# Attention and two MLPs on one core: the second MLP's first layer by seven half products, and one list schedule for both MLPs

## The chip, the cores and the metric

One core of one Trainium2 chip runs the whole program in one launch. The metric is device microseconds (us) of that core. The core has five engines with a queue each, worked off in order: TensorE (PE, matmuls, with weight loads as PEld), VectorE (DVE), ScalarE (ACT), GpSimd (POOL) and SyncE (SP, which issues the DMAs here). Matmuls write PSUM, eight banks of 128 partitions x 512 floats; GpSimd works on SBUF alone.

## The reference

q, k and v are float32; the weights come as float64, in words of 8 bytes, which the kernel turns into floats itself.

```python
attn_out = softmax(q @ k.T / 8, causal) @ v          # 2 batches, 12 heads, 448 tokens, 64 wide
x = attn_out as (896 tokens, 768)
g = x @ w_gate;  val = x @ w_val                     # 768 -> 1536
x2 = (g * sigmoid(g) * val) @ w_out                  # 1536 -> 768
h = x2 @ w_in                                        # 768 -> 2048, moe2_w_in
out = (h * clip(h + 3, 0, 6) / 6) @ moe2_w_out       # 2048 -> 768
```

## The kernel before

**Precision.** Every MLP operand is split in two parts of a reduced float type, a high one (CAST on ScalarE) and the rest (a subtraction on VectorE or GpSimd, `parts_of`). A product of two operands is then three matmuls: high x high, high x low, low x high (`mm3`). The weights come as float64 words: a load of 768 KB lands in `raw`, a Prelu on ScalarE turns the high words, a shift and a join on VectorE (`floats`) finish the float, and a split follows (`unit`).

**Stages.** Attention comes first (up to about 117 us). Then, in the transposed layout (features on partitions, tokens along the free axis, 448 tokens of each batch):

- *Gate and value layers of the first MLP.* Two blocks f of 128 features are done plainly (`plain`). The other ten go by Winograd's form of Strassen's method: the 2 x 2 block matrix has gate and value as its upper and lower half and the two halves of the 768 inputs as columns; the 2 x 2 block operand has the input halves as rows and the two batches as columns. In place of eight half products there are seven (`products`, 9 matmuls of 448 columns each). The weights' sums (s1 to s4) are made per block by `operands`, the tokens' sums (t1 to t4) once. The seven results are combined through sums in banks x, y, z, w and in SBUF tiles (u2, u3, v2), then SiLU and gate (`gate`).
- *w_out*, 432 matmuls: per 128 output features two banks, for tokens 0 to 383 and 384 to 895 (`PARTS`). The results are split into x2h, x2l.
- *w_in* of the second MLP, 16 blocks f of 128 features in plain form, 36 matmuls each: per block one bank of 384 and one of 512 columns; ScalarE makes the relu r, VectorE multiplies and splits (g2h, g2l).
- *w2_out*, two halves of 384 output features, 336 matmuls of 384 columns each: seven banks of 128 tokens, added up over 16 blocks; the last two pairs of blocks run token by token, so that copies and stores begin early.

**What sets the order.** From the plain blocks to w_out the operations are handed to a planner (`Plan.op`, with a cost per engine that may do it) and put in an order by a list schedule (`Plan.run`): the matmuls and the loads in the order written, everything else by when it can start and when the matmuls need it; where `vec` and `pool` may both do it, the schedule picks. Operations marked `port` (all inputs in SBUF) do not overlap each other in the plan. The emitted order is then fixed. w_in and w2_out are issued by loops behind the plan (`next_unit`, `last_layer`), ordered by the framework's own scheduler with raised priority for the work on a bank.

**Names in rows.** L53 is the helper through which all ordered engine calls go, so most rows have that line: go by tiles. `mm` is a PSUM bank, `x`, `t`, `x2` are token operands, `a`, `s` weight operands of the seven products, `whi`/`wlo` those of plain products, `tmp` the SBUF sums, `w`/`v` weights as floats, `gh`/`gl`, `g2h`/`g2l` the split gated results.

Of the kernel before, what the change touches and what calls it, by code (L numbers as in the profile page):

```python
# [8 lines left out]
F32 = mybir.dt.float32  # L9
# [25 lines left out]
EARLY = 0  # L35
SOON = 200
# [124 lines left out]
def tile_attention_glu_mlp(  # L161
# [126 lines left out]
    OUT_ORDER = [(0, 0), (1, 0), (0, 1), (1, 1)] + [(e, hh) for e in range(2, KD) for hh in range(2)]  # L288
    for e, hh in OUT_ORDER:
        rows = w_out[hh * KD * 128 : (hh + 1) * KD * 128]  # L290
        units.append((cols(rows, e), KD, 128))
    for f in range(K2):
        units.append((cols(w2_in, f), KD, 128))
    for eh in range(2):
        for g in range(K2 // 2):
            rows = w2_out[g * 256 : (g + 1) * 256]
            units.append((cols(rows, eh, EH), 2, EH))
# [5 lines left out]
    used = [0]  # L303

    def prefetch(n):
        while len(made) < min(n, len(units)):
            for step in w_unit(*units[len(made)]):
                step()

    def next_unit():  # L310
        u = used[0]
        prefetch(u + 1 + AHEAD)
        used[0] += 1
        got = made[u]
        made[u] = None
        return got

# [13 lines left out]

    PARTS = (slice(0, NT - 512), slice(NT - 512, NT))
# [326 lines left out]
    def mlps():  # L659
        in_attention.clear()  # L660
        more.append(ctx.enter_context(tc.tile_pool(name="more", bufs=1)))
        tmp = ctx.enter_context(tc.tile_pool(name="tmp", bufs=3))
# [3 lines left out]
        def whole(dt, name):  # L666
            return slot([128, NT], dt, name)

        def side(size, name):
            return tmp.tile([128, size], F32, tag=f"sg{size}", name=name, bufs=2 if size == 512 else 1)  # L670

        BATCH = [slice(b * S, (b + 1) * S) for b in range(B)]
        plan = Plan()
        PE448, PE384, PE512 = 0.2005, 0.1735, 0.2275
# [26 lines left out]
        def floats(src, name):  # L701

            raw = ring_spot("raw", [128, KD, 128, 2], U32, "raw")
            w = ring_spot("w", [128, KD, 128], F32, name)
# [63 lines left out]
        temps = [take([128, 2, S], F32, f"tmp{i}") for i in range(3)]  # L768
        ta, tb, sg = temps
# [4 lines left out]
        def gate(f, b, bank_, in0, in1):  # L774

            whole_f, hi, lo = g1[f]
            mid = lambda t: t[:, BATCH[b]]
            m = {"vec": 0.63}
            if whole_f is not None:
                combine(m, at(whole_f, b, mid), in0, in1, ALU.mult)  # L780
                return
            tok = lambda t: t[:, :S]
            combine(m, at(bank_, None, tok), in0, in1, ALU.mult)
            parts_of(at(bank_, None, tok), at(hi, b, mid), at(lo, b, mid), S, both=False, port=False)

        def g_tiles(f):
            if f < EARLY:
                g1[f] = None, take([128, NT], F32R, f"gh{f}"), take([128, NT], F32R, f"gl{f}")
            else:
                g1[f] = take([128, NT], F32, f"g{f}"), None, None  # L790

        def g_parts(f):
            src = g1[f][0]
            hi, lo = take([128, NT], F32R, f"gh{f}"), take([128, NT], F32R, f"gl{f}")
            for part in PARTS:
                mid = lambda t, part=part: t[:, part]
                parts_of(at(src, None, mid), at(hi, part.start, mid), at(lo, part.start, mid), part.stop - part.start)
            g1[f] = None, hi, lo
            give(src)

# [21 lines left out]
        def operands(f):  # L822

            wg, wv = floats(cols(w_gate, f), "w"), floats(cols(w_val, f), "v")
# [13 lines left out]
            combine(either, a21, a11, a21, ALU.subtract, port=True)  # L838
            piece("s3", a21)
# [3 lines left out]
            piece("a12", a12)  # L843
            combine(either, a12, a12, s2, ALU.subtract, port=True)
            piece("a22", a22)
# [3 lines left out]
        def unit(src, both=False):  # L849

            w = floats(src, "w")
            hi, lo = (ring_spot("ws", [128, KD, 128], F32R, n) for n in ("whi", "wlo"))
            parts_of(at(w), at(hi), at(lo), KD * 128, both=both)
            return hi, lo

        def plain(f, ws):

            g_tiles(f)
            for b in range(B):
# [13 lines left out]
                gate(f, b, got[1][0], at(got[1][0], None, tok), at(sg, b, nth(b)))  # L873
# [3 lines left out]
        used[0] += 2  # L877
        for f in range(1, PLAIN):
            plain(f, [unit(cols(w, f), both=True) for w in (w_gate, w_val)])
# [13 lines left out]
        p1, u2, u3, v2 = at(ta, 0, nth(0)), at(ta, 1, nth(1)), at(tb, 0, nth(0)), at(tb, 1, nth(1))  # L893
        add = {"vec": 0.63}
        for f in range(PLAIN, K1):
            a = operands(f)
            g_tiles(f)
            (x, nx), (z, nz), (y, ny), (w, nw) = (bank_spot() for _ in range(4))
            X, Y, Z, W = (at(t, None, tok) for t in (x, y, z, w))
            products(x, a["a11"], b11, True)  # L900
            plan.op(
                {"act": 0.54}, lambda e, x=x: e.copy(p1[2](ta()), tok(x())), reads=[x], writes=[p1[:2]]
# [21 lines left out]
        for f in range(EARLY, K1):  # L924
            g_parts(f)
        x2s = [tuple(take([128, NT], F32R, f"x2{p}{e}") for p in "hl") for e in range(KD)]
        pts = {}
        for u, (e, hh) in enumerate(OUT_ORDER):
# [18 lines left out]
            if hh == 0:  # L947
                continue
# [110 lines left out]
```

## Time and profile before

| | us |
|---|---|
| three runs | 601.73, 604.72, 604.35; median 604.35 |
| the profiled execution, whole | 602.2 |
| its span, first to last instruction | 600.4 |
| mean granted TensorE clock | 0.999 of full speed |

Busy time is given as a share of the span; engines overlap, so the shares add up to more than one, and matmuls are pipelined, so that a matmul's row is longer than the distance to the next. The chain of work that ended last is followed back from the last instruction; where a chain's piece is one engine alone, that engine was never waiting there.

### The profile page before, as it was taken

To read this page: it belongs to the slowest core of one execution; us is meant where nothing else is said; L and a number is where in the kernel's file an instruction comes from. 1 tells how busy PE (TensorE), PEld (TensorE's weight loads), DVE (VectorE), ACT (ScalarE), POOL (GpSimd) and SP (SyncE) were. 2 spreads that over 40 slices of the span, in tenths; PEclk is the share of its full clock that TensorE was granted. 3 is DMA by queue.
4 is the path that set the end of the run, shared out by engine and by line. 5 is a ranking of instruction groups with operands and counts; after the bars stand their busy time and mean duration, and the time that the engine had idled before them with its cause. 6 is when DMAs were issued, how large, how long until landed. Compare 5 with 4: busy or idle time off the path is not lost.

```text
span 600.4 us, 9398 instructions
## 1 busy us (share of the span) xinstructions
PE 593.0 (99%) x3528; PEld 551.0 (92%) x3528; DVE 372.3 (62%) x771; ACT 297.1 (49%) x536; POOL 176.7 (29%) x141
## 2 busy tenths in 40 slices
PE   8999999999999999999999999999999999999997
PEld 5999999989899999999999988888888899999997
DVE  6888889788999998879775434555555522223001
ACT  5788787775554555467344234555555532222000
POOL 4555555140343542363000012222222222223200
PEclk9999999999999999999999999999999999999999
DMA  9555546063333453342566333333343344341002
GB/s 180 131 136 131 133 116 176 7 204 106 105 107 106 149 161 111 106 139 76 163 201 211 105 106 106 105 106 105 106 109 109 108 128 120 112 136 62 1 0 94
DMA packets 83918, 70.15 MB, mean 117 GB/s; under 512 B 35232, under 2 KB 79776, under 8 KB 83872
## 3 DMA queue, kind: packets, MB, share of 16 engines
q1 hardware_dynamic: 83872, 69.55, 40.0%
q8 instruction: 28, 0.46, 0.3%
q14 instruction: 18, 0.15, 0.1%
HBM read 61.73 MB, written 2.75 MB: 107 GB/s over the span
## 4 chain that ended last, share of the span: by engine, by line
PE 94%; DVE 4%; ACT 1%; DMA 0%; issue 0%; POOL 0%; SPq 0%; ACTq 0%; DVEq 0%
PE mm L53 78%; PE pv L574 5%; PE sc L503 4%; PE tp L546 3%; PE tr L428 1%; DVE e L516 1%; DVE qq L441 1%; PE tr L608 1%; DMA kn<-in_k_dram 0%; POOL wlo L53 0%; DVE xn L587 0%; PE zero L367 0%; DVE et L552 0%; PE tr L458 0%; ACT L53 0%
## 5 line engine op out<-in xcount | busy, mean ns | idle before, releaser
L53 POOL TENSOR_TENSOR wlo<-w,whi 128x768 fp32r<-128x768 f32 (+1 forms) x33 | 59.1, 1791 | 257.5 <-PE mm L53 233.1
L53 DVE TENSOR_SCALAR w<-w 128x768 uint32<-128x768 uint32 (+1 forms) x59 | 35.6, 604 | 79.6 <-ACT w L53 76.6
L53 PE MATMUL mm<-whi,g2l 128*128 128x384 f32 x224 | 74.8, 334 | 0.0
L53 PE MATMUL mm<-whi,g2h 128*128 128x384 f32 x224 | 74.8, 334 | 0.0
L53 PE MATMUL mm<-wlo,g2h 128*128 128x384 f32 x224 | 74.8, 334 | 0.0
L574 PE MATMUL pv<-v,et 112*112 112x65 f32 x480 | 73.7, 242 | 0.0
L53 ACT CAST whi<-w 128x768 fp32r<-128x768 f32 (+1 forms) x49 | 40.1, 819 | 66.5 <-PE mm L53 57.4
L53 PE MATMUL mm<-x2h,wlo 128*128 128x384 f32 (+1 forms) x192 | 69.9, 364 | 0.0
L53 PE MATMUL mm<-x2l,whi 128*128 128x384 f32 (+1 forms) x192 | 69.8, 364 | 0.0
L53 PE MATMUL mm<-x2h,whi 128*128 128x384 f32 (+1 forms) x192 | 69.6, 362 | 0.0
L574 PEld LDWEIGHTS pv<-v,et 112*112 112x112 f32 x480 | 65.6, 177 | 1.2
L53 ACT ACTIVATE w<-raw 128x768 f32<-128x768 f32 (+1 forms) x59 | 52.5, 891 | 28.6 <-POOL wlo L53 19.4
L546 PE MATMUL tp<-ident,e 112*112 112x112 f32 x240 | 60.5, 260 | 1.7 <-ACT e L526 1.1
L526 ACT ACTIVATE e<-e,m 112x336 f32<-112x336 f32 (+1 forms) x96 | 48.8, 530 | 19.4 <-DVE m L516 18.4
L53 DVE SCALAR_TENSOR_TENSOR w<-raw,w 128x768 uint32<-128x768 uint32 (+1 forms) x59 | 57.3, 971 | 0.8
L53 PE MATMUL mm<-t,s 128*128 128x448 f32 x270 | 57.0, 366 | 0.0
L53 PEld LDWEIGHTS mm<-t,s 128*128 128x128 f32 x270 | 50.5, 188 | 4.9 <-DVE s L53 0.9
L53 PE MATMUL mm<-gh,wlo 128*128 128x384 f32 (+1 forms) x144 | 52.5, 364 | 0.0
L53 PE MATMUL mm<-gl,whi 128*128 128x384 f32 (+1 forms) x144 | 52.4, 364 | 0.0
L53 PE MATMUL mm<-gh,whi 128*128 128x384 f32 (+1 forms) x144 | 52.2, 362 | 0.0
L516 DVE CUSTOM_DVE_ANT_0 e<-sc,mask 112x336 f32<-112x336 f32 (+1 forms) x96 | 40.7, 446 | 5.2 <-PE sc L503 3.6
L53 PEld LDWEIGHTS mm<-whi,g2h 128*128 128x128 f32 x224 | 42.0, 188 | 0.0
(120 smaller groups left out, 1272.4 us busy)
## 6 DMA issues: line engine op xcount, KB each, us to landing
raw<-in_moe_w_out_dram SPq DMA_DIRECT2D x28, 768.0 KB, 4.3
raw<-in_moe_w_in_dram SPq DMA_DIRECT2D x16, 768.0 KB, 4.5
raw<-in_moe_w_gate_dram SPq DMA_DIRECT2D x12, 768.0 KB, 4.3
raw<-in_moe_w_val_dram SPq DMA_DIRECT2D x12, 768.0 KB, 5.9
kn<-in_k_dram SPq DMA_DIRECT2D x24, 112.0 KB, 2.6
qn<-in_q_dram SPq DMA_DIRECT2D x24, 112.0 KB, 2.7
v<-in_v_dram SPq DMA_DIRECT2D x12, 224.0 KB, 3.1
out_dram<-ob SPq DMA_DIRECT2D x14, 192.0 KB, 1.8
```

The lines of the kernel that those rows point to most:

```text
L53: ins = call(*args, **kw)
L428: nc.tensor.transpose(tr[:, c * C : (c + 1) * C], n[:, c].rearrange("p j d -> p (j d)"), ident[:C, :C])
L441: nc.vector.tensor_copy(hi[r, j, :], f[r, :])
L503: nc.tensor.matmul(sp[:C, o : o + w], t["qq"][:, j, c * C : (c + 1) * C], t[("kk", "k2")[i]][:, j, 0:w], start=(i == 0), stop=(i == 1),)
L516: nc.vector.tensor_tensor_reduce(out=es, in0=sp[:C, o : o + w], in1=mask[:, S - w :], op0=ALU.add, op1=ALU.min, scale=-SCALE, scalar=3.0e3 ...
L526: nc.scalar.activation(out=es, in_=es, func=AF.Exp, scale=-1.0, bias=m[:, x : x + 1])
L546: nc.tensor.transpose(tp[:C, at - lo : at - lo + C], e[:, at : at + C], ident[:C, :C])
L574: nc.tensor.matmul(box["o"][:, qc, :], et[:, at : at + C], vt[:, j, c, :], start=(c == 0), stop=(c == qc))
L608: nc.tensor.transpose(tr[:, c * C : (c + 1) * C], xn[:, c].rearrange("p j d -> p (j d)"), ident[:C, :C])
```

## The change

- **w_in by seven products.** Blocks 2f and 2f + 1 take the place of gate and value: 8 pairs of 7 products, each 9 matmuls of 448 columns. The sums t1 to t4 and the blocks b11, b21, b22 of x2 are made as w_out's banks end (`turned`), for which w_out's banks now hold 448 tokens of a batch each and its output blocks come in pairs e, e + 3. The gated results are kept as floats (`h`) and split later (`whole_parts`), since SBUF has no room for both parts beside the operands.
- **Sums in PSUM.** One function `seven` does both layers. ScalarE copies the first product from bank x into bank y, TensorE adds product s2 x t2 on top; ScalarE copies that sum to bank z and to u2, TensorE adds s3 x t3 and later a22 x t4 onto z. VectorE is left with two adds (W + u2, and v2 = Z + v2). The first product of the next block, a11, is issued between s3 and a22 of the present one.
- **One plan to the end.** w_in and w2_out, copies and stores are planned too. Four groups of w2_out's matmuls (`fill`) stand between s3 and a22 of the last pair.
- Splits may go to either engine in more places (`both`), and the splits of the first four gated blocks are let into the gate layers (`FEW`).

The core of the diff (the planner's class and attention are untouched):

```diff
+        def seven(n, source, sets, tiles, near, far, fill=None):
+
+            b11, b21, b22, (t1, t2, t3, t4) = *sets[:3], sets[3:]
...
+            ahead = begin(0)
+            for f in range(n):
+                a, x, nx = ahead
+                (y, ny), (z, nz), (w, nw) = (bank_spot() for _ in range(3))
+                Z, W = (at(t, None, tok) for t in (z, w))
+
+                def p6():
+                    products(y, a["s2"], t2, False)
+                    bank_copy(z, y)
+                    bank_copy(u2, y)
+
+                def p5():
+                    products(w, a["s1"], t1, True)
+                    bank_copy(v2, w)
+
+                bank_copy(y, x)
+                for step in (p5, p6) if f == 0 else (p6, p5):
+                    step()
+                products(x, a["a12"], b21, False)
+                near(f, x)
+                products(z, a["s3"], t3, False)
+                if f + 1 < n:
+                    ahead = begin(f + 1)
+                elif fill:
+                    idle.extend((nx, ny))
+                    fill()
+                combine(add, W, W, u2, ALU.add)
+                combine(add, v2, Z, v2, ALU.add)
+                products(z, a["a22"], t4, False)
+                far(f, 0, y, z)
+                products(w, a["s4"], b22, False)
+                far(f, 1, y, w)
...
-            products(x, a["a11"], b11, True)
...
-            products(z, a["s3"], tk[3], True)
-            products(y, a["s2"], tk[2], True)
-            combine(add, u2, Y, p1, ALU.add)
-            combine(add, u3, Z, u2, ALU.add)
-            products(w, a["s1"], tk[1], True)
-            combine(add, v2, W, u3, ALU.add)
-            products(x, a["a12"], b21, False)
-            silu(at(sg, 0, nth(0)), x)
-            products(z, a["a22"], tk[4], False)
-            combine(add, Z, Z, u2, ALU.add)
-            gate(f, 0, z, Z, at(sg, 0, nth(0)))
-            products(w, a["s4"], b22, False)
-            combine(add, W, W, u2, ALU.add)
...
+        def relu_far(f, b, y, t):
+            if b:
+                gated(2 * f, 1, at(sg, 0, nth(0)), at(t, None, tok))
+            else:
+                gated(2 * f + 1, 1, at(y, None, tok), v2)
+                gated(2 * f + 1, 0, at(sg, 1, nth(1)), at(t, None, tok))
...
+            lambda f: (cols(w2_in, 2 * f), cols(w2_in, 2 * f + 1)),
...
-        for f in range(K2):
-            wh, wl = next_unit()
...
-                mm3(pt, [(wh[:, i], wl[:, i], x2[i][0][:, part], x2[i][1][:, part]) for i in range(KD)])
```

Three places show how the order moves. The first is TensorE in w_in: before, a run of one block (its bank of 384 columns ends, its bank of 512 begins), and after, the same layer from a pair's product s3 to its a22. In the names `x` is a token operand there (x2, t or b blocks alike), `s` and `a` the weights' parts; the numbers tell buffers apart.

```order
L53 MATMUL mm_4183<-x2h_4029,whi 128x384
L53 MATMUL mm_4183<-x2l_4034,whi 128x384
L53 MATMUL mm_4183<-x2h_4029,wlo 128x384
L53 MATMUL mm_4207<-x2h_3575,whi 128x512
L53 MATMUL mm_4207<-x2l_3584,whi 128x512
L53 MATMUL mm_4207<-x2h_3575,wlo 128x512
```

```order
L52 MATMUL mm_4432<-x_3957,s_4332 128x448 x3
L52 MATMUL mm_4432<-x_4158,s_4332 128x448 x3
L52 MATMUL mm_4475<-x_3603,a_4400 128x448 x2
L52 MATMUL mm_4475<-x_3603,a_4400 128x448 [waits DVE_49]
L52 MATMUL mm_4475<-x_3787,a_4400 128x448 x3
L52 MATMUL mm_4475<-x_4059,a_4400 128x448 x3
L52 MATMUL mm_4432<-x_3730,a_4348 128x448 [waits DVE_49]
L52 MATMUL mm_4432<-x_3730,a_4348 128x448
L52 MATMUL mm_4432<-x_3730,a_4348 128x448 [waits Pool_49]
L52 MATMUL mm_4432<-x_3961,a_4348 128x448 x3
```

Bank 4432 (z) gets product s3, then bank 4475 the next pair's a11, then z again its a22, whose first matmul waits for VectorE; before, no matmul came back to a bank that another engine had to read first.

The second is VectorE in w_in: before, one block's gate and split between the conversions of the weights, and after, somewhat more than half of a pair's round.

```order
L53 SCALAR_TENSOR_TENSOR mm_4123<-r_4142,mm_4123 128x384 [waits Activation_49]
L53 TENSOR_TENSOR g2l_4122<-mm_4123,g2h_4121 128x384 [waits Activation_49]
L53 SCALAR_TENSOR_TENSOR mm_4147<-r_4166,mm_4147 128x512 [waits Activation_49]
L53 TENSOR_SCALAR w<-w 128x768 [waits Activation_49]
L53 TENSOR_TENSOR g2l_4122<-mm_4147,g2h_4121 128x512 [waits Activation_49]
L53 SCALAR_TENSOR_TENSOR w<-raw,w 128x768 [waits DMAHW4_49,DVE_49]
```

```order
L52 TENSOR_TENSOR mm_4543<-mm_4543,tmp_2280 128x448 [waits Activation_49]
L52 SCALAR_TENSOR_TENSOR h_4592<-tmp_2045,mm_4475 128x448 [waits Activation_49]
L52 TENSOR_TENSOR tmp_2280<-mm_4553,tmp_2280 128x448 [waits PE_49]
L52 TENSOR_TENSOR s_4607<-w,s_4607 128x384 [waits Activation_49]
L52 SCALAR_TENSOR_TENSOR h_4620<-mm_4503,tmp_2280 128x448 [waits Activation_49]
L52 TENSOR_TENSOR s_4625<-s_2162,s_4625 128x384 [waits PE_49,Activation_49]
L52 TENSOR_TENSOR s_2162<-v 128x384 [waits DVE_49,Pool_49]
L52 TENSOR_SCALAR w<-w 128x768 [waits Activation_49]
L52 TENSOR_TENSOR a_4640<-w,a_4640 128x384 [waits Activation_49]
L52 SCALAR_TENSOR_TENSOR h_4620<-tmp_2045,mm_4553 128x448 [waits Activation_49]
L52 TENSOR_TENSOR s_4658<-s_2162,s_4658 128x384 [waits Activation_49]
L52 SCALAR_TENSOR_TENSOR h_4592<-tmp_2045,mm_4543 128x448 [waits Activation_49]
```

The third row after is the add v2 that reads bank z and for which a22 waits; the row ahead of it is the gate of the pair's first block, which waits for ScalarE's relu of bank x. The round goes on with a join, a shift, a split, a join and starts again.

The third is VectorE in the gate layers, from one block's joins to the next splits, before and after.

```order
L53 TENSOR_TENSOR tmp_2258<-mm_2743,tmp_2258 128x448 [waits PE_49]
L53 SCALAR_TENSOR_TENSOR v<-raw,v 128x768 [waits DMAHW7_49,DVE_49]
L53 TENSOR_TENSOR tmp_2299<-mm_2727,tmp_2258 128x448 [waits DVE_49]
L53 TENSOR_TENSOR tmp_2299<-mm_2758,tmp_2299 128x448 [waits DVE_49,PE_49]
L53 TENSOR_TENSOR a_2774<-w,a_2774 128x384 [waits Activation_49]
L53 TENSOR_TENSOR v<-w,v 128x384 [waits Pool_49]
```

```order
L52 TENSOR_TENSOR mm_2638<-mm_2638,tmp_2280 128x448 [waits Activation_49]
L52 TENSOR_TENSOR s_2671<-s_2162,s_2671 128x384 [waits Activation_49]
L52 TENSOR_TENSOR v<-w,v 128x384 [waits DVE_49]
L52 TENSOR_TENSOR s_2686<-s_2162,s_2686 128x384 [waits PE_49,Activation_49]
L52 TENSOR_TENSOR tmp_2280<-mm_2650,tmp_2280 128x448 [waits PE_49]
```

The three sums u2, u3 and v2 ahead of a22 have become the one add v2; W + u2, which came after product s4, now comes ahead of it.

## Rows read from the trace of the kernel before

**Rows 1.** The page, part 1: busy us, share of the span, instructions.

```profile
PE 593.0 (99%) x3528; PEld 551.0 (92%) x3528; DVE 372.3 (62%) x771; ACT 297.1 (49%) x536; POOL 176.7 (29%) x141
```

**Rows 2.** The chain that ended last, its final pieces: start us, us, what.

```profile
125.88 37.87 PE mm L53 x182
...
163.78 433.15 PE mm L53 x2236
...
597.01 0.56 DVE ob L53
```

**Rows 3.** Timeline of PE, first matmul of w_out, w_in, w2_out: start us, us.

```profile
276.80 0.34 PE L53 MATMUL mm<-gh,whi 128*128 128x384 f32 x1
...
363.98 0.33 PE L53 MATMUL mm<-x2h,whi 128*128 128x384 f32 x1
...
480.25 0.33 PE L53 MATMUL mm<-whi,g2h 128*128 128x384 f32 x1
```

**Rows 4.** Groups by line and shape, PE in w_in: count, busy us, mean ns.

```profile
L53 PE MATMUL mm<-x2h,wlo 128*128 128x512 f32 x96 | 37.7, 392 | 0.0
```

**Rows 5.** Timeline of PE in the gate layers, products of a later block.

```profile
202.02 5.63 PE L53 MATMUL mm<-t,s 128*128 128x448 f32 x27
207.49 1.99 PE L53 MATMUL mm<-x,a 128*128 128x448 f32 x9
209.31 1.99 PE L53 MATMUL mm<-t,a 128*128 128x448 f32 x9
...
220.26 1.99 PE L53 MATMUL mm<-x,a 128*128 128x448 f32 x9
```

**Rows 6.** Timeline of PE in the gate layers, an early block.

```profile
157.60 2.02 PE L53 MATMUL mm<-t,a 128*128 128x448 f32 x9
159.46 2.02 PE L53 MATMUL mm<-x,s 128*128 128x448 f32 x9
...
163.18 5.94 PE L53 MATMUL mm<-t,s 128*128 128x448 f32 x27
```

**Rows 7.** Busy us in stretches: length, PE, PEld, DVE, ACT, POOL; clock, DMA.

```profile
207.49:220.26 12.77, 12.77 (x65) 11.83 (x63) 12.08 (x20) 6.63 (x13) 5.77 (x5) 1.00 0.41 127
363.98:480.25 116.27, 116.27 (x578) 104.38 (x577) 59.66 (x95) 60.75 (x95) 29.52 (x16) 1.00 0.37 107
```

**Rows 8.** Groups by shape on DVE: adds from PSUM, splits, joins, shifts.

```profile
L53 DVE SCALAR_TENSOR_TENSOR w<-raw,w 128x768 uint32<-128x768 uint32 x57 | 56.2, 985 | 0.8
...
L53 DVE TENSOR_SCALAR w<-w 128x768 uint32<-128x768 uint32 x57 | 34.9, 613 | 79.5 <-ACT w L53 76.6 <-issue 2.8
...
L53 DVE TENSOR_TENSOR tmp<-mm,tmp 128x448 f32<-128x448 f32 x30 | 18.6, 620 | 4.8 <-PE mm L53 4.0
...
L53 DVE TENSOR_TENSOR s<-s,s 128x384 fp32r<-128x384 f32 x17 | 9.3, 546 | 0.0
```

**Rows 9.** Groups by shape on POOL: a split, a sum.

```profile
L53 POOL TENSOR_TENSOR a<-v,a 128x384 fp32r<-128x384 f32 x9 | 11.3, 1261 | 10.3 <-ACT a L53 7.0 <-issue 3.3
...
L53 POOL TENSOR_TENSOR s<-v 128x384 f32<-128x384 f32 x5 | 5.1, 1017 | 1.0 <-DVE v L53 1.0
```

**Rows 10.** Groups by shape on ACT: conversion, relu, cast, copy from PSUM.

```profile
L53 ACT ACTIVATE w<-raw 128x768 f32<-128x768 f32 x57 | 51.4, 902 | 28.6 <-POOL wlo L53 19.4 <-DMA raw<-in_moe_w_out_dram 6.2 <-DMA raw<-in_moe_w_in_dram 1.3
...
L53 ACT ACTIVATE r<-mm,half 128x512 f32<-128x512 f32 x16 | 11.1, 691 | 24.1 <-PE mm L53 24.1
...
L53 ACT CAST s<-s 128x384 fp32r<-128x384 f32 x20 | 10.2, 512 | 2.7 <-DVE s L53 2.7
...
L53 ACT COPY tmp<-mm 128x448 f32<-128x448 f32 x10 | 5.3, 530 | 5.6 <-PE mm L53 5.5
```

**Rows 11.** Timelines of DVE and POOL around a late add.

```profile
204.98 1.77 DVE L53 SCALAR_TENSOR_TENSOR w<-raw,w 128x768 uint32<-128x768 uint32 x1
206.68 0.61 DVE L53 TENSOR_TENSOR tmp<-mm,tmp 128x448 f32<-128x448 f32 x1
...
204.88 1.05 POOL L53 TENSOR_TENSOR s<-w,s 128x384 fp32r<-128x384 f32 x1 [2.79 <-ACT s L53]
```

More of the change, by code (lines that the diff above doesn't have):

```diff
@@ L287, in tile_attention_glu_mlp @@
         units.append((cols(w_val, f), KD, 128))
[L288 to L291, printed above, removed]
-    for f in range(K2):
[L293 to L297, printed above, removed]
+    OUT_ORDER = [(0, 0), (3, 0), (0, 1), (3, 1), (1, 0), (1, 1), (4, 0), (4, 1), (2, 0), (5, 0), (2, 1), (5, 1)]
     made = []
@@ L772, in mlps, with gate, whole_parts @@
         g1 = {}
[L774 to L798, printed above, removed]
+        def gate(f, b, in0, in1):
+            combine({"vec": 0.63}, at(g1[f], b, lambda t: t[:, BATCH[b]]), in0, in1, ALU.mult)
+        def whole_parts(src, name):
+            hi, lo = take([128, NT], F32R, name + "h"), take([128, NT], F32R, name + "l")
+            for b in range(B):
+                mid = lambda t, b=b: t[:, BATCH[b]]
+                parts_of(at(src, b, mid), at(hi, b, mid), at(lo, b, mid), S)
             give(src)
+            return hi, lo
         tok = lambda t: t[:, :S]
@@ L927, in mlps, with copy @@
+        def copy(dst, src):
+            plan.op({"act": 0.54}, lambda e: e.copy(dst[2](dst[0]()), src[2](src[0]())), reads=[src[:2]], writes=[dst[:2]])
         pts = {}
[L928 removed]
+        for e, hh in OUT_ORDER:
             if hh == 0:
[L930 to L935 removed]
+                pts[e] = [bank_spot() for _ in range(B)]
+            wh, wl = unit(cols(w_out[hh * KD * 128 : (hh + 1) * KD * 128], e))
+            for b in range(B):
+                pt = pts[e][b][0]
@@ new lines, in mlps, with gated @@
+            idle.extend((n0, n1))
+        give(*(t for i in range(KD, K1) for t in g1[i]))
+        g2 = {}
+        def gated(f, b, r, h):
+            o = g2[f]
+            plan.op(
+                {"act": 0.56},
+                lambda e: e.activation(
+                    out=r[2](r[0]()), in_=h[2](h[0]()), func=AF.Relu, scale=1.0 / 6.0, bias=half[:, 0:1]
+                ),
+                reads=[h[:2]], writes=[r[:2]],
+            )
+            plan.op(
+                {"vec": 0.65},
+                lambda e: e.scalar_tensor_tensor(
+                    out=o()[:, BATCH[b]], in0=r[2](r[0]()), scalar=1.0, in1=h[2](h[0]()),
+                    op0=ALU.min, op1=ALU.mult,
+                ),
+                reads=[r[:2], h[:2]], writes=[(o, b)],
+            )
```

275 lines of the change are left out of this document (150 added, 125 removed).

## The prediction

> **What bounds the kernel now.** First the busy shares: TensorE is busy 99% of the span, VectorE 62%, ScalarE 49%, GpSimd 29% [rows 1]. A busy share of TensorE alone proves nothing, so next the chain that ended last. Its last long piece is 2236 matmuls in a row, from 163.78 us for 433.15 us, with no other engine in between, and after it one copy of 0.56 us and the store [rows 2]. From 163.78 us to the end the time is therefore a count of matmuls times their spacing, and whatever takes matmuls out of that piece without making TensorE wait comes off the end one for one. Third, where the stages lie in that piece: w_out begins at 276.80, the first layer of the second MLP (w2_in) at 363.98, w2_out at 480.25 [rows 3]. w2_in thus lasts 116.27 us and w_out 87.18. Fourth, the first MLP's gate and value layers, which already run by seven half products: one block f, 63 matmuls of 448 columns, goes from 207.49 to 220.26 (from one a12 product to the next), 12.77 us or 0.2027 each, and TensorE shows no gap there although VectorE was busy 12.08 of the 12.77 us and GpSimd 5.77 [rows 5, 7]. That block is the model for the new stage.
>
> **The change, part by part.**
>
> *w2_in by seven products.* Before, 6 groups of 96 matmuls (the row shown, its two partners and the same three at 384 columns) are 576 [rows 4]. After, 8 pairs of blocks take 7 products of 9 matmuls of 448 columns: 504. At the spacing of the block above, 504 x 0.2027 = 102.2 us in place of 116.27: **-14.1 us**.
>
> *w_out at 448 + 448 columns in place of 384 + 512.* The count stays 432: 432 x 0.2027 = 87.6 against 87.18 now: **+0.4 us**.
>
> *The spacing itself.* At 448 columns the trace has two. The product that starts at 157.60 has its successor 1.86 us later, 0.2067 a matmul; the one at 207.49 has it 1.82 later [rows 5, 6]. Between them lies a wait of TensorE: the 27 matmuls that begin at 163.18 last 5.94 us, those from 202.02 last 5.63. So the spacing seems to be reset by a wait, and which one the new stages get is not shown. If all of w_out, w2_in and the roughly 530 later matmuls of the gate layers ran at the longer one, (432 + 504 + 530) x 0.004 = 5.9 us would be lost; if none, nothing. I take a quarter, **+1.5 us**, since most of the present trace at 448 columns is in the short one.
>
> *Sums kept in PSUM.* A block of the gate layers loses three VectorE adds (0.620 each) and gains three ScalarE copies (0.530) [rows 8, 10]. VectorE there falls from 12.08 to about 10.2 us of 12.77, ScalarE rises from 6.63 to 8.2 [rows 7]: both under TensorE's 12.77, so nothing on the path: 0. With four of the g splits moved in between, a bit of VectorE's gain is spent again.
>
> *What w2_in's pairs ask of the other engines.* VectorE's order (shown in the change) has in one round 6 adds or gates from PSUM (6 x 0.620), 2 shifts (0.613), 2 joins (0.985), 5 splits and one sum of 384 columns (6 x 0.546): 3.72 + 1.23 + 1.97 + 3.28 = 10.2 us. GpSimd has 2 splits (1.261) and 3 sums (1.017): 5.6 us. ScalarE has 4 copies (0.530), 7 casts (0.512), 2 conversions (0.902) and 4 relus; a relu of 512 columns takes 0.691, a copy of 448 0.530, so 0.6: 2.1 + 3.6 + 1.8 + 2.5 = 10.0 us [rows 8 to 10]. All below 12.77, but no longer by much: until now this stage had VectorE at 59.66 of 116.27 us, which was cover that cost nothing [rows 7].
>
> *The new wait.* Product a22 adds onto the bank z, which VectorE must have read for v2 after product s3. Between s3 and a22 now stands one product, a11 of the next block: 1.82 us. The add takes 0.62, so VectorE may come 1.1 us late before TensorE waits; behind a waiting a22 stand s4 and the whole next block. Before, the same bank had two products of cover. How late VectorE comes: in the block shown the add that needed the product ended at about 205.8 (18 of the 27 from 202.02, and the 0.17 that a matmul's row lasts beyond its spacing) starts at 206.68, 0.85 late, because a join ahead of it took 1.77 us where the mean is 0.985; it had met a GpSimd operation that ran from 204.88 to 205.93 [rows 8, 11]. So 0.85 late is the normal bad case, and one more such collision (0.8) would make TensorE wait 0.5. With 18 blocks in both layers: from 0 to 18 x 0.5 = 9 us. I take **+2 us**, nearer to nothing, because the gate layers lose three adds per block, and because in w2_in VectorE's instruction before the add waits for the relu of a12's product, which ends a product ahead of s3.
>
> The Trainium skill, SBUF — State Buffer, section Who interferes with whom, states that a VectorE instruction with two SBUF inputs and a GpSimd instruction that reads SBUF exclude each other for a whole instruction. The 1.77 us join agrees with it. By that rule the pair's shared work is serial (rival 1 has what that gives).
>
> *Seams.* Out of w_out: the last half of x2 that product s2 needs takes an add (0.62), a cast and, on GpSimd, a split, which by the rows of 384 columns last 0.6 and 1.5 us at 448: 2.7 us after the last w_out matmul [rows 8 to 10]; ahead of it stand a11, s1 and seven matmuls of s2, 25 x 0.203 = 5.1 us. Covered: 0. Into w2_out: the last a22 has twelve matmuls of 384 columns as cover, more columns than the usual nine of 448; the splits of h0 have four products. At the end of the program the copy and the store stay as they are. Taken as 0; if one of these covers fails, 1 to 3 us.
>
> *Loads.* The same tensors in as many pieces. On SP's queue four of w2_out's loads now stand behind the first half's seven stores, where two stood; they serve the last four of the second half's eight pairs, which begin half of a 58 us half later (w2_out's two halves take 480.25 to 597 [rows 2, 3]), so some 29 us are there for a load and its conversion: 0.
>
> Sum, against the profiled execution (span 600.4, its own time 602.2): 600.4 - 14.1 + 0.4 + 1.5 + 2.0 = 590.2, and with the same 1.8 outside the span **592 us**. The median of the three runs, 604.35, lies 2.1 above the profiled time, the lowest 0.5 below; I take the profiled one as base and leave 2 us for this in the range.
>
> **Rivals.**
>
> 1. *VectorE and GpSimd pace the pairs.* Of VectorE's 10.2 us, 6.5 are instructions with all inputs in SBUF; with GpSimd's 5.6 that is 12.1 us that cannot overlap, of 12.77. For it: the collisions in rows 11, and queues in fixed order that wait for each other (ScalarE's ten us too). Against: the block of rows 7 ran with VectorE at 12.08 and GpSimd at 5.77 and TensorE did not wait. If a pair took 13.5 us, 8 x 0.73 = 5.8 us more than without any wait: 590.2 - 2.0 + 5.8 + 1.8 = 596.
>
> 2. *The long spacing throughout.* All 448-column stages at 0.2067: 592 + 4.4 = 596. For it: the 182 matmuls ahead of the chain's long piece took 37.87 us, 0.208 each [rows 2]. Against: since the wait at 163 us the short one holds, also at 220 us [rows 5, 6].
>
> 3. *Slower than before.* Two old blocks take 2 x 7.27 = 14.53 us; from there on a pair gains nothing. It takes rival 1's mechanism at 14.9 us per pair: 8 x (14.9 - 12.77) = 17 us above the bare count: about 605. VectorE would have to stand idle or blocked 4.7 of 14.9 us in each round, for waits on ScalarE's casts and relus. Nothing in the model block shows half of that.
>
> 4. *A seam fails* and costs about 3 us: 595.
>
> **How the numbers follow.** Forecast (588 to 594) 0.58; rival 1 (594 to 601) 0.20; rival 2 0.12; rival 4 0.06; rival 3 0.04. Range: below, no spacing loss and no waits, 588.6, and a run at the low end of the three, 588; above, rival 1 and 2 up to 599. About 0.5% (3 us) is what a measurement of this kernel can tell from no change. Faster takes all but rival 3 and the top of rival 1: 0.92; same 0.04; slower 0.04.
>
> **What will show it.** Right: the matmuls number 3456 in place of 3528; w2_in lasts 102 to 105 us; the long piece of the chain holds some 2160 matmuls with few breaks; VectorE's busy share in w2_in rises from 51% to about 80%. The term of the spacing is read from the distance of product starts, 1.82 or 1.86. Rival 1 shows as TensorE waiting for VectorE once per pair at a22, and a pair of 13 us or more; rival 4 as a single gap at either end of w2_in. The forecast is wrong if gaps of half a microsecond repeat in every block.

## The result, and the profile after

The changed kernel takes 588.79 us (median of 4 runs, 588.15 to 588.98), the kernel before 603.45 (4 runs): ratio 0.9757, 95% interval 0.9728 to 0.9786. The forecast was 592.0, its range 588 to 599. The profiled execution has a span of 586.4 us and 1.8 us around it.

Part 1 of the page, to be read beside [rows 1]: 73 matmul records fewer (one is missing of 3456), VectorE and ScalarE busier, GpSimd a little less.

```profile
PE 577.8 (99%) x3455; PEld 544.1 (93%) x3456; DVE 420.5 (72%) x842; ACT 343.8 (59%) x653; POOL 167.3 (29%) x149
```

The chain that ended last, as in [rows 2]. Two long pieces of TensorE alone, with one interruption, in which the chain goes through VectorE:

```profile
126.19 138.30 PE mm L52 x681
264.59 0.96 DVE wlo L52
...
272.07 0.55 DVE tmp L52
272.66 310.22 PE mm L52 x1626
582.96 0.56 DVE ob L52
```

The timeline of TensorE where stages begin, to compare with [rows 3]: first matmul of the MLPs, gate layers by seven products, the late a22, w_out, w_in, the first fill of w2_out, w_in's last a22 and s4, w2_out for good.

```profile
116.78 0.64 PE L52 MATMUL mm<-x,whi 128*128 128x448 f32 x2
...
147.58 1.99 PE L52 MATMUL mm<-x,a 128*128 128x448 f32 x9
...
272.66 2.11 PE L52 MATMUL mm<-t,a 128*128 128x448 f32 x9 [0.88 <-DVE tmp L52]
...
276.43 0.36 PE L52 MATMUL mm<-g0h,whi 128*128 128x448 f32 x1
...
363.98 1.99 PE L52 MATMUL mm<-x,a 128*128 128x448 f32 x9
...
462.48 0.34 PE L52 MATMUL mm<-whi,h0h 128*128 128x384 f32 x1
...
464.58 2.02 PE L52 MATMUL mm<-x,a 128*128 128x448 f32 x9
466.44 2.02 PE L52 MATMUL mm<-x,s 128*128 128x448 f32 x9
468.30 0.34 PE L52 MATMUL mm<-whi,h0h 128*128 128x384 f32 x1
```

From these starts and the same ones of the kernel before comes a ledger. w_in's 102.22 us are 468.30 - 363.98 without the 2.10 that the fill takes from 462.48 to 464.58; the fill counts in the last line.

| us | before | after | change |
|---|---|---|---|
| up to the first MLP matmul | 117.02 | 116.78 | -0.24 |
| plain blocks | 31.28 | 30.80 | -0.48 |
| gate layers by seven | 128.50 | 128.85 | +0.35 |
| w_out | 87.18 | 87.55 | +0.37 |
| w_in | 116.27 | 102.22 | -14.05 |
| w2_out and the end | 120.17 | 120.17 | 0.00 |
| span | 600.42 | 586.37 | -14.05 |

The busy time of a gate block, of a pair of w_in, and of w_in up to the fill, in the columns of [rows 7]. TensorE has no gap in any of the three; the pair takes 12.77 us, as the block of the kernel before did.

```profile
207.77:220.54 12.77, 12.77 (x64) 11.84 (x63) 10.55 (x18) 8.07 (x17) 3.58 (x3) 1.00 0.39 124
376.75:389.52 12.77, 12.77 (x65) 11.83 (x63) 9.92 (x15) 9.00 (x18) 6.56 (x6) 1.00 0.43 123
363.98:462.48 98.50, 98.50 (x488) 91.30 (x486) 79.04 (x120) 74.11 (x139) 44.20 (x40) 1.00 0.39 119
```

What TensorE waits for in the MLPs is two lines (us in total, times, longest); each wait also lengthens the next spacing by 0.11.

```profile
PE mm L52 <- DVE tmp L52: 0.9, 1, 0.9
PE mm L52 <- POOL wlo L52: 0.6, 1, 0.6
```

The first is the a22 at 272.66, in the last block of the gate layers. VectorE's timeline there, and at the same add v2 of a pair of w_in:

```profile
270.17 0.62 DVE L52 TENSOR_TENSOR mm<-mm,tmp 128x448 f32<-128x448 f32 x1
270.70 1.37 DVE L52 SCALAR_TENSOR_TENSOR w<-raw,w 128x768 uint32<-128x768 uint32 x1
272.00 0.61 DVE L52 TENSOR_TENSOR tmp<-mm,tmp 128x448 f32<-128x448 f32 x1
...
386.07 0.62 DVE L52 TENSOR_TENSOR tmp<-mm,tmp 128x448 f32<-128x448 f32 x1 [0.48 <-PE mm L52]
```

In the pair VectorE stands ready and idle, 0.48 us, until s3 has ended (384.05 + 1.99 = 386.04), begins 0.03 later and is done at 386.69, 1.00 us before a22 begins at 387.69. So it is in all nine gate blocks that have a next one and in the seven such pairs: the add begins 0.03 to 0.16 us behind s3, and 0.88 to 1.00 us are left. The last gate block has no next block, so no a11 stands between s3 and a22, and there TensorE waits.

### The profile page after: what moved, and what is told of

Read it like the earlier page. It is cut to its first block, busy times and chain, and to the rows that moved or that the text cites. A ratio compares the mean times of both kernels' runs of the same rounds, so it can differ in the third digit from the quotient of the medians.

```text
span 586.4 us, 9458 instructions
## 1 busy us (share of the span) xinstructions
PE 577.8 (99%) x3455; PEld 544.1 (93%) x3456; DVE 420.5 (72%) x842; ACT 343.8 (59%) x653; POOL 167.3 (29%) x149
## 4 chain that ended last, share of the span: by engine, by line
PE 92%; DVE 4%; issue 1%; POOL 0%; DMA 0%; ACT 0%; SPq 0%; DVEq 0%; POOLq 0%; ACTq 0%
PE mm L52 76%; PE pv L547 5%; PE sc L476 4%; PE tp L519 3%; PE tr L401 1%; DVE e L489 1%; DVE qq L414 1%; DVE w L52 1%; PE tr L581 1%; POOL wlo L52 0%; DMA qn<-in_q_dram 0%; DVE et L525 0%; DVE xn L560 0%; SPq L375 0%; PE zero L340 0%
## 5 line engine op out<-in xcount | busy, mean ns | idle before, releaser
L52 PE MATMUL mm<-x,a 128*128 128x448 f32 x396 | 86.3, 365 | 0.0
L52 PE MATMUL mm<-x,s 128*128 128x448 f32 x378 | 81.0, 365 | 0.0
L52 PEld LDWEIGHTS mm<-x,a 128*128 128x128 f32 x396 | 74.4, 188 | 5.9
L52 PEld LDWEIGHTS mm<-x,s 128*128 128x128 f32 x378 | 71.0, 188 | 5.6
L52 DVE TENSOR_TENSOR wlo<-w,whi 128x768 fp32r<-128x768 f32 x27 | 25.8, 955 | 34.0 <-PE mm L52 32.6
L519 PEld LDWEIGHTS tp<-ident,e 112*112 112x112 f32 x240 | 36.3, 153 | 3.4 <-ACT e L499 1.8
L415 POOL TENSOR_TENSOR k<-f,kk 64x448 fp32r<-64x448 f32 x22 | 27.5, 1251 | 35.4 <-DVE kk L414 34.5
L52 ACT COPY mm<-mm 128x448 f32<-128x448 f32 x36 | 18.7, 518 | 30.0 <-PE mm L52 29.9
L476 PE MATMUL sc<-k,qq 128*112 128x336 f32 (+1 forms) x96 | 34.9, 366 | 0.0
L476 PE MATMUL sc<-kk,qq 128*112 128x336 f32 (+1 forms) x96 | 34.7, 369 | 0.1
```

Source lines behind the costliest of these rows:

```text
L52: ins = call(*args, **kw)
L415: nc.gpsimd.tensor_tensor(out=lo[lr, j, :], in0=f[r, :], in1=hi[r, j, :].bitcast(F32), op=ALU.subtract)
L476: nc.tensor.matmul(sp[:C, o : o + w], t["qq"][:, j, c * C : (c + 1) * C], t[("kk", "k2")[i]][:, j, 0:w], start=(i == 0), stop=(i == 1),)
L519: nc.tensor.transpose(tp[:C, at - lo : at - lo + C], e[:, at : at + C], ident[:C, :C])
```

## The experiments

Attention is untouched, but its end moves from profile to profile (the MLPs' first matmul lies between 116.8 and 119.1 us), which is as much as some effects looked for. So beside the times the table gives what the traces show from that first matmul to the end, and its parts: gate layers by seven, w_out, w_in and all behind it ("rest"). The stretches are those of one profiled execution each. "Before, beside it" is the median of the kernel before, run together with that kernel: it moves by 1.5 us, so medians of different rows differ by as much without any edit.

| kernel | time, median (runs: lowest to highest) | before, beside it | first to end | gate | w_out | rest |
|---|---|---|---|---|---|---|
| before | 603.45 (4: 601.73 to 604.72) | | 483.40 | 128.50 | 87.18 | 236.44 |
| changed | 588.79 (4: 588.15 to 588.98) | 603.45 | 469.60 | 128.85 | 87.55 | 222.39 |
| e9_plain_in | 603.02 (10: 602.71 to 607.09) | 602.62 | 484.13 | 128.85 | 87.55 | 236.91 |
| e4_old_in | 589.60 (4: 588.88 to 590.66) | 602.62 | 470.21 | 128.85 | 87.55 | 222.99 |
| e5_old_both | 594.40 (4: 593.61 to 596.38) | 602.62 | 477.61 | 134.41 | 89.28 | 223.06 |
| e10_old_both_order | 595.20 (4: 592.65 to 597.20) | 602.42 | 477.51 | 133.89 | 89.28 | 223.06 |
| e12_old_both_few0 | 595.34 (1) | 602.42 | 475.80 | 132.13 | 89.28 | 223.09 |
| e6_no_pool | 588.63 (4: 588.57 to 588.79) | 602.62 | 469.75 | 128.85 | 87.55 | 222.54 |
| e3_no_cover | 658.99 (1) | 601.91 | 539.94 | 157.30 | 87.56 | 264.25 |
| e1_s4_first | 587.66 (6: 587.25 to 593.82) | 601.91 | 468.43 | 127.68 | 87.55 | 222.37 |
| e2_s4_vec | 587.34 (4: 587.22 to 587.82) | 601.91 | 468.44 | 127.68 | 87.55 | 222.39 |
| e11_both_waits | 586.73 (6: 586.22 to 592.99) | 602.42 | 467.57 | 127.68 | 87.56 | 222.39 |
| e7_one384 | 588.64 (1) | 601.91 | 469.79 | 128.85 | 87.73 | 222.40 |
| e13_few0 | 592.82 (1) | 602.42 | 473.43 | 129.02 | 89.28 | 224.32 |

**Is it the count of matmuls?** e9_plain_in takes the seven products out of w_in and leaves everything else.

```diff
-        seven(
-            K2 // 2,
...
-            relu_tiles, relu_near, relu_far, fill,
-        )
+        for f in range(K2):
+            wh, wl = unit(cols(w2_in, f))
+            g2[f] = take([128, NT], F32, f"h{f}")
+            for b in range(B):
+                t, n = bank_spot()
...
+                    lambda e, t=t, wh=wh, wl=wl, xk=xk: mm3(
+                        tok(t()),
+                        [(wh()[:, k], wl()[:, k], x()[:, 0], x()[:, 1]) for k, x in enumerate(xk)],
+                    ),
...
+                gated(f, b, at(sg, b, nth(b)), at(t, None, tok))
```

> w_in in plain form again (576 matmuls of 448 columns, 16 blocks), with everything else of the change: the gate layers with sums in PSUM, one plan to the end. Theory: the whole gain is the count of matmuls: 72 x 0.2027 = 14.6 us back, span 601.0 us, within 1 us of the kernel before (600.4). Rival: the plan and the sums in PSUM have a part of the gain by themselves: span under 599.

Its ratio to the kernel before is 1.0019 (0.9998 to 1.004), its span 601.0. The rest grows by 14.52 us, the 72 matmuls at 0.2027 are 14.6. The chain has one piece to the end:

```profile
272.78 324.72 PE mm L52 x1698
```

So the gain is the count; against the kernel before, the plan to the end and the sums in PSUM have no part of it that could be measured.

**Are the sums in PSUM needed?** e4_old_in has the old sums in w_in, e5_old_both in both layers. This is the edit within `seven`, taken where `old` is set:

```diff
+                    bank_copy(u2, x)
+                    products(z, a["s3"], t3, True)
+                    products(y, a["s2"], t2, True)
+                    combine(add, u2, Y, u2, ALU.add)
+                    combine(add, v2, Z, u2, ALU.add)
+                    products(w, a["s1"], t1, True)
+                    combine(add, v2, W, v2, ALU.add)
+                    products(x, a["a12"], b21, False)
...
+                    products(z, a["a22"], t4, False)
+                    combine(add, Z, Z, u2, ALU.add)
+                    products(w, a["s4"], b22, False)
+                    combine(add, W, W, u2, ALU.add)
```

> In w_in alone the sums are made as in the kernel before (five adds on VectorE, one copy on ScalarE, in place of two adds and three copies); a11 of the next pair stays ahead. Per pair VectorE goes from 9.92 to about 11.8 us of 12.77, ScalarE from 9.0 to 7.4. Theory: as long as VectorE stays under 12.77 TensorE doesn't see it (before, the gate block ran with VectorE at 12.08): span 586.4 to 587.5 us. Rival (VectorE and GpSimd pace the pairs, for waits between the queues and work that can't overlap): a pair of 13.3 us or more, span 590.5 or more.

> Both layers with the old sums on VectorE, the rest as changed. Theory: the sums in PSUM bring nothing by themselves, and without them the last gate block has cover for its a22 again: span 585.3 to 586.5 us. Rival: without them VectorE falls behind in both layers, 0.3 us or more per block, span 592 or more.

In w_in of e4_old_in TensorE has no gap and the stretch is 98.50 us, as in the changed kernel. The schedule gave more work to GpSimd, so that VectorE is hardly busier (79.7 us, GpSimd 59.5 in place of 44.2):

```profile
364.76:463.26 98.50, 98.50 (x488) 91.19 (x486) 79.69 (x123) 62.10 (x114) 59.52 (x53) 1.00 0.28 87
```

What e4_old_in loses, 0.6 us, is one gap at the seam into w2_out. e5_old_both loses 8.0 us in its profiled execution, the longest of its four runs: 5.6 in the gate layers, 1.7 in w_out, where the spacing is 0.2067, and the seam. Its new waits were for operand s3, which `operands` makes fifth and the old products need second; e10_old_both_order puts it second, as before, and e12_old_both_few0 also takes the four early splits out (`FEW = 0`).

> As e5_old_both, but the weights' operands are made in the order in which the old products need them (s3 second, as in the kernel before; in e5_old_both they came in the order of the new products, s3 fifth). Theory: the 8 us of e5_old_both come from s3's operands being late, not from VectorE's three more adds: the waits on s are gone, span 585.2 to 586.8 us. Rival: VectorE has too much in the gate layers with the old sums and the four splits that were let in: at least 3 us of waits stay, span 589 or more.

> As e10_old_both_order, and none of the gated blocks' splits let into the gate layers. Theory: with the splits behind the gate layers VectorE has room for the old sums: no waits in the gate layers, but w_out's start waits for the splits, 0 to 3 us: span 585 to 589. Rival: waits in the gate layers stay as in e10_old_both_order, if it has any.

Both theories fell: the order of the operands is not it (133.89), and without the early splits 4.5 us over the wait-free 127.68 of e1_s4_first are left (132.13). Whether those splits are part of it is open, since e12_old_both_few0 has one run, within the 4.6 us over which e10_old_both_order's four spread. The gate layers of e10_old_both_order in the columns of [rows 7], what TensorE waits for there, two pieces of the chain ahead of the wait at 256.96, and the VectorE join that ends 0.06 us before the first of them begins:

```profile
148.76:282.65 133.89, 130.21 (x631) 117.74 (x630) 124.88 (x177) 70.99 (x134) 64.25 (x53) 1.00 0.36 113
```

```profile
PE mm L52 <- DVE s L52: 3.5, 3, 1.8
```

```profile
246.79 5.52 DMA raw<-in_moe_w_gate_dram
...
255.70 3.04 DVE s L52 x3
```

```profile
245.78 0.95 DVE L52 SCALAR_TENSOR_TENSOR w<-raw,w 128x768 uint32<-128x768 uint32 x1
```

VectorE is busy 93% here. Read along the chain: VectorE's join frees the load buffer at 246.73, the next load begins at 246.79 and lands at 252.31, and the operands made from it come too late for s3. That the join itself was late for want of VectorE's time is argued, not shown. The last piece has a second cause, which no run separates from the first: GpSimd is at work beside VectorE's splits. The split that s3's low part comes from, in the gate layers of e10_old_both_order and then of the changed kernel (count, busy us, mean ns):

```profile
L52 DVE TENSOR_TENSOR s<-v,s 128x384 fp32r<-128x384 f32 x9 | 12.4, 1381 | 0.0
...
L52 DVE TENSOR_TENSOR s<-v,s 128x384 fp32r<-128x384 f32 x9 | 4.9, 549 | 0.2 <-ACT s L52 0.2
```

The same split takes 0.83 us longer in every block. Ahead of the wait at 256.96 two splits in a row last 1.38 and 1.35 us, 1.6 more than two at 0.55, and that wait is 1.63 us longer than the spacing.

Before, the same layers held 128.50 us with the old sums and VectorE at 115.66 us. The three kernels with old sums have a11 one block ahead and two temporaries where the kernel before had a11 in its own block and three temporaries; which of these, or of the other parts of the change, makes the difference wasn't tried. Shown is: in the changed order the gate layers lose 4.5 to 6.7 us against 127.68 without the sums in PSUM, of which 0.5 to 1.8 are matmuls at 0.2067 and the rest waits; w_in itself loses nothing.

**Does GpSimd's part help or hinder?** e6_no_pool gives all of w_in's operands to VectorE (`fill` is passed for w_in alone).

```diff
-            either = {"vec": 0.52, "pool": 1.1}
+            either = {"vec": 0.52} if alone else {"vec": 0.52, "pool": 1.1}
...
-                a = operands(*source(f))
+                a = operands(*source(f), alone=bool(fill))
...
-                parts_of(src, at(t, 0, nth(0)), at(t, 1, nth(1)), HD * 128)
+                parts_of(src, at(t, 0, nth(0)), at(t, 1, nth(1)), HD * 128, both=not alone)
```

> In w_in GpSimd gets none of the splits and sums of the weights, VectorE all of them. VectorE per pair: 9.92 us and about 5 more instructions of 0.55 us that GpSimd had, 12.7 to 13.2 us. Theory: VectorE becomes the bound, a pair takes 13.2 to 13.8 us, 8 x 0.4 to 1.0 us, span 590 to 595 us. Rival: what costs VectorE is the collisions with GpSimd; without them its instructions get shorter, a pair stays at 12.77 us, span 586.4.

The rival was right: the time is the same, and w_in has no gap. VectorE took over 35 instructions and is busy only 8.0 us more, 87.0 in place of 79.0:

```profile
364.34:462.84 98.50, 98.50 (x488) 91.27 (x486) 87.00 (x155) 73.27 (x139) 8.14 (x6) 1.00 0.37 111
```

Two groups by shape on VectorE in w_in, first of the changed kernel, then of e6_no_pool (count, busy us, mean ns):

```profile
L52 DVE TENSOR_TENSOR a<-w,a 128x384 fp32r<-128x384 f32 x12 | 10.8, 901 | 0.8 <-ACT a L52 0.5
...
L52 DVE TENSOR_TENSOR s<-w,s 128x384 fp32r<-128x384 f32 x6 | 6.4, 1070 | 0.0
```

```profile
L52 DVE TENSOR_TENSOR a<-w,a 128x384 fp32r<-128x384 f32 x14 | 7.8, 555 | 1.9 <-ACT a L52 1.8
...
L52 DVE TENSOR_TENSOR s<-w,s 128x384 fp32r<-128x384 f32 x7 | 3.9, 556 | 0.4 <-ACT s L52 0.3
```

The same split takes 901 or 1070 ns on the mean beside GpSimd and 555 alone. Row by row, 14 of VectorE's instructions in w_in of the changed kernel, each of them beside one of GpSimd, last 9.4 us longer in all than the shortest of their shape; in e6_no_pool it is three, 1.6 us. So of the 19.3 us that the 35 instructions take at 0.55, 7.8 come back as collisions that are gone, and VectorE's rows add up to 11.6 us more. (Its busy time rises less, by 8.0, because neighbouring rows overlap a little and an overlap counts once.) The Trainium skill, SBUF — State Buffer, section Who interferes with whom, says that a VectorE instruction with two SBUF inputs and a GpSimd instruction that reads SBUF lock each other out for a whole instruction; these means (901 and 1070 ns against 555) agree.

**What does a22's cover carry?** e3_no_cover moves a11 of the next block ahead of s3; e1_s4_first gives the last gate block its product s4 as cover.

```diff
+                if f + 1 < n:
+                    ahead = begin(f + 1)
                 products(z, a["s3"], t3, False)
-                if f + 1 < n:
-                    ahead = begin(f + 1)
-                elif fill:
+                if f + 1 == n and fill:
```

```diff
+                late = f + 1 == n and not fill
+                if late:
+                    products(w, a["s4"], b22, False)
                 products(z, a["a22"], t4, False)
                 far(f, 0, y, z)
-                products(w, a["s4"], b22, False)
+                if not late:
+                    products(w, a["s4"], b22, False)
```

> a11 of the next block goes ahead of s3, so that a22 stands right behind s3 in 16 of the 18 blocks (9 of the gate layers, 7 of w_in). Theory: then each of these waits for the end of s3 and VectorE's add, as the last gate block does now: about 0.98 us each (a matmul's row lasts 0.17 beyond its spacing, VectorE starts 0.04 later, the add takes 0.62, the restart 0.15), 16 x 0.98 = 15.7 us, span about 602. Rival, the reasoning of the prediction: VectorE often comes 0.85 us late on top, then up to 1.8 us each, span 610 or more. If the a22 waited less than 0.5 us each (span under 594), the cover would not be what decides.

> Only the last block of the gate layers changes: its product s4 goes ahead of a22, which there has no product of a next block ahead of it. Theory: that missing cover is the whole of the one long wait of the changed kernel (a22 starts 1.05 us late at 272.66 us, and 0.11 us is lost again on the matmul behind it); s4 then covers it, the wait is gone and the span goes from 586.4 to about 585.3 us. Rival: VectorE is simply behind at this place (two joins and splits stand in its queue), s4 waits for its own sum W + u2 instead and nothing is gained: span 586.3 to 586.8.

e3_no_cover cost 70.3 us, not 15.7 (and its rival, a VectorE that is 0.85 us late, put no more than 1.8 us on a block). The chain, block by block in the gate layers:

```profile
173.84 13.05 PE mm L52 x63
187.59 13.04 PE mm L52 x63
201.34 13.04 PE mm L52 x63
215.07 13.05 PE mm L52 x63
230.78 14.60 PE mm L52 x63
249.61 15.66 PE mm L52 x63
```

From 187.59 to 201.34 a block takes 13.75 us, 0.98 more than 12.77, which is the expected price. From the block at 215.07 on, and in w_in, it takes 15.7 to 20.1 (but for the last gate block, whose a22 comes 0.9 late), for two reasons. The first is VectorE's fixed order: the plan put the add v2 behind operands whose casts ScalarE can't begin before s3 has ended. Around 437 us (PE, DVE, ACT rows of the timeline):

```profile
435.03 1.99 PE L52 MATMUL mm<-x,s 128*128 128x448 f32 x9
441.35 3.73 PE L52 MATMUL mm<-x,a 128*128 128x448 f32 x9 [4.34 <-DVE tmp L52]
...
437.59 0.56 DVE L52 TENSOR_TENSOR s<-w,s 128x384 fp32r<-128x384 f32 x1 [4.74 <-ACT s L52]
...
440.68 0.62 DVE L52 TENSOR_TENSOR tmp<-mm,tmp 128x448 f32<-128x448 f32 x1
...
437.05 0.51 ACT L52 CAST s<-w 128x384 fp32r<-128x384 f32 x1 [4.53 <-PE mm L52]
```

s3 ends at 437.02, yet the add begins at 440.68: a cast, a split, a gate, two splits and a shift come first. The second is TensorE's clock. The nine matmuls at 441.35 last 3.73 us, at 0.373 spacing. The stretch of the first six waits, and two stretches behind later ones (the column ahead of the DMA share is the granted clock):

```profile
158.85:230.78 71.93, 65.52 (x318) 58.78 (x316) 63.98 (x100) 46.63 (x91) 26.10 (x21) 1.00 0.43 137
...
287.09:292.85 5.76, 5.76 (x15) 5.12 (x16) 3.35 (x5) 1.79 (x3) 0.56 (x1) 0.50 0.00 0
441.35:446.40 5.05, 5.05 (x14) 4.48 (x15) 3.40 (x5) 1.66 (x3) 2.16 (x2) 0.50 0.46 138
```

Through the waits of 1.1 to 2.2 us between starts the granted clock stayed at 2.4 GHz; behind each of the ten pauses of 3.0 to 5.1 us it was at 1.2 GHz for the next 3 to 6 us. Why the plan put the add there wasn't followed up. The edit also hands the plan the next block's operands ahead of s3, so the 70.3 us are the price of this order, not of the missing cover alone.

In e1_s4_first the wait is gone: gate layers 127.68 in place of 128.85, which is 630 matmuls at 0.2027. The times don't show it: the median is 1.1 us lower, but that of the kernel before beside it is 1.5 us lower too.

e2_s4_vec and e11_both_waits also go for the other wait, at 125 us, for a subtraction on GpSimd. e2_s4_vec moved the wrong one (of plain block 1, for which nothing waits); in e11_both_waits it is the value weights of block 0, made at attention's end.

```diff
-            split_w(hi[:, p], lo[:, p], w[:, p])
+            split_w(hi[:, p], lo[:, p], w[:, p], by=vec if pieces == 1 else None)
```

> The edit of e1_s4_first, and the low part of the value weights of plain block 1 always on VectorE, where TensorE waited 0.75 us at 125.2 us for GpSimd's 1.83 us subtraction. Theory: VectorE's takes 0.95 us, TensorE's wait falls by about 0.7 us, span 584.6 us. Rival: VectorE has other work in front at that time, the wait stays: 585.3. Beyond this the spacing of the 448 column matmuls after the wait could come out as 0.2067 in place of 0.2027 when this wait is another: then about 1.0 us more for the matmuls up to the next wait or change of size, or up to 5.5 us if it holds for all of the stages behind.

> The edit of e1_s4_first, and the subtraction that TensorE waits for at 125 us (the low part of plain block 0's value weights, which e2_s4_vec did not touch) on VectorE, which is idle there from 121.95 to 125.13 us. Theory: VectorE makes it in 0.95 us from 124.25, before TensorE needs it; the wait of 0.75 us and the 0.11 us behind it go, the span from the first w_out matmul back is unchanged: about 584.4 us, time 586.8. Rival: VectorE's next conversions come later by it and TensorE waits a few matmuls on: 585.3.

e2_s4_vec is as e1_s4_first: the wait stayed. In e11_both_waits TensorE does not wait at all from attention's end:

```profile
122.00 461.19 PE mm L52 x2371
```

From the first MLP matmul to the end it takes 467.57 us, 2.03 less than the changed kernel, as expected. Its own profile begins the MLPs at 119.11, so its span (586.7) hides that; four of its other five runs have spans of 584.4 to 585.0, as expected. The median is 586.73, the ratio to the kernel before 0.9749 (0.9713 to 0.9785). By its stages it is the best version here; by times alone it can't be told from the changed kernel, since the intervals overlap.

**What sets the spacing?** e7_one384 puts one matmul of 384 columns ahead of w_out (its result is overwritten); e13_few0 was meant for the splits (`FEW = 0` in the changed kernel).

```diff
+            if (e, hh) == OUT_ORDER[0]:
+                pt, hi = pts[e][0][0], g1[0][0]
...
+                    lambda e, pt=pt, hi=hi, wh=wh: ten.matmul(
+                        pt()[:, :384], wh()[:, 0], hi()[:, :384], start=True, stop=True
+                    ),
```

> One extra matmul of 384 columns ahead of the first matmul of w_out (its result is overwritten), all else as in the changed kernel. Theory: the spacing of the 448 column matmuls is a state that a wait or a matmul of another size sets and that then holds: behind it w_out and w_in up to the next 384 column matmuls (some 918 matmuls) run at 0.2067 in place of 0.2027, 3.7 us, plus 0.17 for the matmul itself: span 590.2 us. Rival: the spacing comes from something else, the stages stay at 0.2027: span 586.6 us.

> The changed kernel with none of the gated blocks' splits let into the gate layers. Theory: the splits come at the end of the gate layers, where VectorE has 1.8 us less slack; w_out's first matmuls then take a split each 0.61 us, about what VectorE needs for one (0.62): 0 to 3 us, span 586.4 to 589.4. Rival: the splits are taken in early anyway: 586.4.

The theory of e7_one384 fell: w_out takes 87.73, the matmul itself and nothing more. e13_few0 shows no wait for the splits at w_out's start (its gate layers take 0.17 us more); it lost 1.73 us in w_out and 1.93 behind it. The same 1626 matmuls that took 310.22 us in the changed kernel took

```profile
273.63 313.93 PE mm L52 x1626
```

without a gap: 0.2067 in place of 0.2027 from the wait at 272.55 to w_in's end, which is most of the 4.4 us that rival 2 put on the long spacing. Both kernels had that wait at the same place, 1.25 us between starts in the one, 1.08 in the other. So here the spacing changed at a wait; which one comes, and whether the edit has to do with it, is open, since e13_few0 is a single run.

The spread of the times in the table fits a spacing that differs from run to run, though no profile of such a run is there to show it. An estimate from the numbers above: the long spacing through gate layers, w_out and w_in is 1566 x 0.004 = 6.3 us, and the highest runs of e1_s4_first and e11_both_waits lie 6.4 and 6.3 us above the middle of their other five; from the wait at 271.5 on in e9_plain_in it is 1008 x 0.004 = 4.0 us, and two of its ten runs lie some 4 us above the rest.

## Why the prediction was right, point by point

- **w_in, -14.1.** Measured -14.05, and e9_plain_in gives 14.52 back. Matmuls taken out of a gapless piece come off the end one for one. VectorE's share of w_in is 80% (79.04 of 98.50 us), as forecast; the long piece of the chain has one break, at 264 to 272 us.
- **w_out, +0.4.** Measured +0.37.
- **The spacing, +1.5.** Mis-sized. All stages got 0.2027, but for the 18 matmuls from 464.58 (1.86 us a product). The plain blocks even lost their long one: 31.28 to 30.80. The bounds were right: e13_few0 got the long one in w_out and w_in, 3.66 us. Nothing in the working could tell which one comes, so this term was a bet, and that it came out at next to nothing is luck. The time, 588.79, lies 0.8 above the range's lower end, which stood for no spacing loss and no waits; with the 6.3 us of the estimate above it would have lain inside the range too.
- **The new wait, +2.** Mis-sized, and its place was wrong. The step that failed is "0.85 late is the normal bad case": the late add of [rows 11] had two products of cover, and here, with one, the add comes 0.03 to 0.16 us behind s3 in all 16 blocks. That the list schedule kept VectorE free for it because it was due sooner is argued, not tested. The one wait that there is, 1.17 us with what follows it, stands where the prediction counted a product of cover that isn't there, in the last gate block; e1_s4_first shows it.
- **Sums in PSUM, 0.** Right against the kernel before, whose gate layers had next to no waits. What the prediction missed is that they are needed in the new order (e10_old_both_order, e12_old_both_few0).
- **The pairs' load.** 10.2, 10.0 and 5.6 us for VectorE, ScalarE and GpSimd were forecast, 9.92, 9.00 and 6.56 measured, in 12.77.
- **Seams and loads, 0.** The rest behind w_in's matmuls is 120.17 in both kernels.
- **The sum.** 590.2 was forecast for the span. Of the 3.8 us between it and 586.37, 1.5 are the spacing's term and 0.8 the wait's; the other 1.5 are gains not in the sum: 0.24 ahead of the MLPs, 0.48 in the plain blocks, and 0.82 in the gate layers, where [rows 6] still had the long spacing and a short wait (128.50 against 127.68).
- **Rivals.** 1 (VectorE and GpSimd pace the pairs): no; they do collide, by 9.4 us in w_in, but TensorE's 12.77 stayed the longest, with 1.00 us to spare at a22. 2: not in this kernel, in e13_few0. 3 and 4: no; a seam's gap of 0.6 showed only with the old sums. Slower than before came only with the cover taken away.

## What to carry to other kernels

Where a trace shows one engine in an unbroken piece, a change is worth the instructions that it takes out of that piece, and the work is to make sure that no wait appears; compare stage by stage, from a start that the change doesn't touch. When a wait is covered by work of the next round, look at the last round, which has none. A cover that looks like slack (1.00 us here) can hold much more than its length: in the order without it the fixed queues of three engines waited for one another, and TensorE's granted clock fell to half behind each long pause.

## What the runs showed of the hardware

- A pause costs more than itself: in e3_no_cover, behind ten pauses of 3.0 to 5.1 us between matmul starts, the granted clock was 0.50 (1.2 GHz) for 3 to 6 us, at 0.373 us a matmul of 448 columns in place of 0.203; behind the waits of 1.1 to 2.2 us there it stayed at 1.00 (2.4 GHz).
- The same stream of 448-column matmuls ran at 0.2027 or at 0.2067 us over hundreds of microseconds, changing at waits (e13_few0, 272.55 us) and also without one: in e5_old_both, e10_old_both_order and e12_old_both_few0 it went back to 0.2027 some 2.5 us into w_in. A single matmul of 384 columns didn't change it (e7_one384); behind the fill of w2_out, 12 matmuls of 384, the changed kernel's last 18 of 448 ran at 0.2067.
- A VectorE split of 128x384 took 0.55 us alone and up to 1.38 beside a GpSimd instruction. Giving 35 instructions to GpSimd in w_in relieved VectorE by only 8 us of busy time, since 14 of VectorE's own instructions lasted 9.4 us longer for it; taking them back cost nothing (e6_no_pool).
